# Recomputing xn and y from x for the gradients, LayerNorm of the first part on VectorE, and MLP weights loaded later

## The chip, the cores and the metric

The kernel runs on one core of a Trainium2 chip. The metric is the device time of one execution in microseconds (us); lower is better.

## The reference

A block of a network, forward and backward, in bf16. `xn = LN(x)`; an attention branch and a gated MLP branch both take `xn`; the MLP normalises once more (`y` below), and the result is `x + s * silu(m)`. The kernel returns the output and the gradients of all seven inputs.

```python
def _A_ref(x, wqkv, wo):            # B, S, D = 1, 2048, 512; H = 32 heads of 16
    qkv = (x @ wqkv).reshape(B, S, 3, H, Dh).transpose(2, 0, 3, 1, 4)
    q, k, v = qkv[0], qkv[1], qkv[2]
    scores = jnp.einsum("bhqd,bhkd->bhqk", q, k) * (Dh ** -0.5)
    p = _softmax(scores, axis=-1)
    o = jnp.einsum("bhqk,bhkd->bhqd", p, v)
    return o.transpose(0, 2, 1, 3).reshape(B, S, D) @ wo

def _B_ref(x, w1, b1, w2, b2):      # F = 1792
    y = _layernorm(x, axis=-1)
    h = _gelu(jnp.einsum("bsd,df->bsf", y, w1) + b1)
    return jnp.einsum("bsf,fd->bsd", h, w2) + b2

xn = _layernorm(x, axis=-1)
s = _A_ref(xn, A_wqkv, A_wo)
g = _silu(_B_ref(xn, B_w1, B_b1, B_w2, B_b2))
out = x + s * g                      # and jax.vjp of it with grad_out
```

## The kernel before

The 2048 rows are 16 tiles (t) of 128; four tiles make a group (g, or sc in the MLP). The order of the work on every engine is the order in which the program issues it (`manual_schedule`): each engine, and each queue from which an engine issues its DMAs, goes through its instructions one after the other, and an instruction that waits for a semaphore holds all behind it. The engines are TensorE (PE), VectorE (DVE), ScalarE (ACT), GpSimd (POOL) and SyncE (SP, which only issues DMAs). ScalarE computes and issues DMAs from the same queue.

There are three parts.

*The first part* (`phase_pre`, L37 to L279). SP loads x in four pieces; ScalarE issues the loads of wqkv and w1. `ln1(g)` computes the statistics of a group with `bn_stats` and `bn_aggr` on VectorE, a square root on ScalarE (L87) and a reciprocal on VectorE; `norm` (L91) then makes xn, on VectorE for group 0 and on GpSimd for groups 1 to 3. Group 0 is transposed by TensorE, the others by DMA transposes on SP (L108) into xnT. The loop over 16 tiles (L128) multiplies xnT with wqkv: three PSUM tiles pk, pv, pq per t, which ScalarE casts to NSall and NQ. GpSimd squares k and q (`sq`, L149, four buffers), VectorE sums the squares (L124). NSall has two halves that alternate by group, and each half is stored to NAT_s by SP after its fourth tile, NQ to NATQq_s. The hooks at L127 place `ln1(2)`, `ln1(3)` and the four `ln2` in this loop. `ln2(g)` stores xn to XN_s, makes y from xn, transposes y to yT and stores y to Y_s. At t = 3 ScalarE issues the loads of w2, b1 and b2, at t = 7 SP the transposing load of woT.

Then follows the MLP forward. `h1(sc)` (L185) makes 14 PSUM tiles from w1 and yT; VectorE adds b1 into h1row (six buffers), ScalarE applies gelu into hgT, SP stores every h1row to H1T_s and at the end hgT to HGT_s. `m_step(t)` multiplies hgT with w2 (ps_m), makes the gate and its slope (gB, stored to GB_s), the gradient dso and its projection with woT. Two groups of h1 run ahead of the first m_step.

*The attention core* (`attention_core`, L634) computes forward and backward of the 32 heads and leaves Oall and dQall in SBUF and dKVT_s in DRAM.

*The last part* (`phase3`, L347) makes the output and the gradients. First dWo from Oall and dso (ps_dwo, L434; four copies by ScalarE at L438 through three buffers). Then a loop over 16 tiles (L452): ps_so from oT and wo, two products on VectorE with the two halves of gb (dm_all, t1), the output on GpSimd (`ot`, with the tile xt of x), and dW of q from xn_all and dQall (L469). gb and xt are loaded by ScalarE's queue in `load_gbx`, three buffers each, two tiles ahead:

```python
                if t + 2 < NT:
                    load_gbx(t + 2)
```

xn_all is loaded from XN_s in four pieces before the loop (L428). After it come dW of k and v (L486), db2, and dW2 (L504 to L522), seven chunks of hidden units whose activations hgc are loaded by DMA transposes through two buffers; y_all is loaded from Y_s ahead of it (L501). The gradients through the MLP (`do_D`, `do_E`, with y_all in the LayerNorm backward), through LN (with xn_all) and dW1 (with y_all) end the program.

Of the kernel before, what the change touches and what calls it, by code (L numbers as in the profile page):

```python
# [9 lines left out]
f32 = mybir.dt.float32  # L10
ACT = mybir.ActivationFunctionType
ALU = mybir.AluOpType
# [4 lines left out]
NT = S // 128  # L17
# [19 lines left out]
def phase_pre(tc, k, A_x, A_wqkv, A_wo, B_w1, B_b1, B_w2, B_b2, grad_out):  # L37
    nc = tc.nc
# [3 lines left out]
    with ExitStack() as c1:  # L42
# [24 lines left out]
        with ExitStack() as c0:  # L67
# [7 lines left out]
            for i in (1, 2, 0):  # L75
                nc.scalar.dma_start(out=wqkv_sb[:, :, i * D:(i + 1) * D], in_=wv[:, :, i * D:(i + 1) * D])
            nc.scalar.dma_start(out=w1_sb[:], in_=B_w1.rearrange("(c p) f -> p c f", p=128))
            xn, y, st = {}, {}, {}

            def stats(g, src, rstd_all, tagn):  # L80
                s6 = wk0.tile([128, 4, nc.vector.BN_STATS_DIM], f32, name="ln_st")
                mv = wk0.tile([128, 4, nc.vector.BN_AGGR_DIM], f32, name="ln_mv")
                for i in range(4):
                    nc.vector.bn_stats(out=s6[:, i, :], in_=src[:, i, :])
                    nc.vector.bn_aggr(out=mv[:, i, :], in_=s6[:, i, :])
                rs = rstd_all[:, 4 * g:4 * g + 4]
                nc.scalar.activation(out=rs, in_=mv[:, :, 1], func=ACT.Sqrt, bias=k.eps_t[:], scale=1.0)  # L87
                nc.vector.reciprocal(out=rs, in_=rs)
                return mv, rs

            def norm(eng, dst, src, mv, rs):  # L91
# [3 lines left out]

            def ln1(g):
                src = x_all[:, 4 * g:4 * g + 4, :]
                mv, rs = stats(g, src, k.rstd1, "1")
                xn[g] = p0.tile([128, 4, D], bf16, name="xn", bufs=4)
                norm(nc.vector if g == 0 else nc.gpsimd, xn[g], src, mv, rs)  # L100
                if g == 0:
                    for i in range(4):
                        pt = psT.tile([128, IC, 128], bf16, name="tp_ps", tag="tp")
                        for b in range(IC):
                            nc.tensor.transpose(pt[:, b, :], xn[g][:, i, b * 128:(b + 1) * 128], k.ident_bf[:])
                        nc.scalar.copy(out=xnT[:, i, :, :], in_=pt[:])
                else:
                    nc.sync.dma_start_transpose(out=xnT[:, 4 * g:4 * g + 4].rearrange("c t m q -> c (t m) q"),  # L108
                                                in_=xn[g][:].rearrange("q t c -> q (t c)"))

            def ln2(g):
                nc.sync.dma_start(out=k.XN_s[g * 512:(g + 1) * 512, :].rearrange("(t p) d -> p t d", p=128), in_=xn[g][:])
                mv, rs = stats(g, xn[g], k.rstd2, "2")
                y[g] = p0.tile([128, 4, D], bf16, name="y", bufs=2)
                norm(nc.vector, y[g], xn[g], mv, rs)
                nc.sync.dma_start_transpose(out=yT[:, 4 * g:4 * g + 4].rearrange("c t m q -> c (t m) q"),
                                            in_=y[g][:].rearrange("q t c -> q (t c)"))
                nc.sync.dma_start(out=k.Y_s[g * 512:(g + 1) * 512, :].rearrange("(t p) d -> p t d", p=128), in_=y[g][:])

            sqs = {}  # L120

# [6 lines left out]
            for t in range(NT):  # L128
                i4 = t // 4
                if t % 4 == 0:  # L130
                    NQ = p0.tile([128, NPAIR, 4, 2, DH], bf16, name="NQ", bufs=2)
                ns = NSall[:, i4 % 2]
                ps3 = []
                for i in range(3):
                    off = (1, 2, 0)[i] * D
                    ps = psA.tile([128, 512], f32, name=("pk", "pv", "pq")[i], tag="mm")
                    for ic in range(IC):
                        nc.tensor.matmul(ps[:], lhsT=xnT[:, t, ic, :], rhs=wqkv_sb[:, ic, off:off + D], start=(ic == 0), stop=(ic == IC - 1))
# [4 lines left out]
                nc.scalar.copy(out=kk, in_=as_pairs(ps3[0]))  # L143
                nc.scalar.copy(out=ns[:, :, t % 4, :, 17:33], in_=as_pairs(ps3[1]))
                nc.scalar.activation(out=qq, in_=as_pairs(ps3[2]), func=ACT.Copy, scale=0.25)
                sqs[t] = []
                for dst, v in ((kn2, kk), (qn2, qq)):
                    sq = wk0.tile([128, H, DH], f32, name="sq", bufs=4)
                    nc.gpsimd.tensor_tensor(out=sq[:].rearrange("p (a j) c -> p a j c", j=2), in0=v, in1=v, op=ALU.mult)  # L149
                    sqs[t].append((dst, sq))  # L150
                for f in hooks.get(t, ()):
                    f()
                if t >= 1:
                    reduce_of(t - 1)
                if t % 4 == 3:
                    nc.sync.dma_start(out=k.NAT_s[:, :, t - 3:t + 1, :].rearrange("a p t c -> p a t c"), in_=ns.rearrange("p a t j c -> p a t (j c)"))
                    nc.sync.dma_start(out=k.NATQq_s[:, :, t - 3:t + 1, :].rearrange("a p t c -> p a t c"), in_=NQ[:].rearrange("p a t j c -> p a t (j c)"))
                if t == 3:
                    nc.scalar.dma_start(out=w2_sb[:], in_=B_w2.rearrange("(c p) d -> p c d", p=128))
                    nc.scalar.dma_start(out=b1_bf[:], in_=B_b1.rearrange("(c p) -> p c", p=128))  # L160
                    nc.scalar.dma_start(out=b2_bf[:], in_=B_b2.rearrange("(o d) -> o d", o=1).to_broadcast([128, D]))
                if t == 7:
                    nc.sync.dma_start_transpose(out=woT[:], in_=A_wo)
            reduce_of(NT - 1)
            nc.vector.tensor_copy(out=b1c[:], in_=b1_bf[:])
            nc.vector.tensor_copy(out=b2bc[:], in_=b2_bf[:])
# [10 lines left out]
        with ExitStack() as c0:  # L177
# [77 lines left out]
                m_mm(t)  # L255
            ops0 = pair_loads(nc, k, op0, op0["Pad"], 0)
            first = {9: ops0["plain"], 10: ops0["ck"], 11: ops0["tk"], 12: lambda: ops0["cq"](0, 4), 13: lambda: ops0["tq"](0, 4)}
            load_dot(0)
            load_dot(1)
            h1(0)  # L260
            h1(1)
            row_bound()
            for sc in range(4):
                for t in range(4 * sc, 4 * sc + 4):
                    m_step(t)
                    if t in first:
                        first[t]()
                if sc + 2 < 4:
                    h1(sc + 2)
            gate(NT - 1)  # L270
            slope_out(NT - 3, nc.gpsimd)
            slope_out(NT - 2, nc.gpsimd)
# [74 lines left out]
def phase3(ctx, tc, k, A_x, A_wqkv, A_wo, B_w1, B_w2, grad_out, out_0, out_1, out_2, out_3, out_4, out_5, out_6, out_7):  # L347
# [5 lines left out]
    with ExitStack() as c1:  # L353
# [23 lines left out]
        with ExitStack() as c2:  # L377
# [643 lines left out]
def full_kernel(ctx, tc, A_x, A_wqkv, A_wo, B_x, B_w1, B_b1, B_w2, B_b2, grad_out,  # L1021
# [9 lines left out]
    nc.vector.memset(k.eps_t[:], EPS)  # L1031
    k.rstd1 = persist.tile([128, NT], f32, name="rstd1")
    k.rstd2 = persist.tile([128, NT], f32, name="rstd2")
    k.ones_bf = persist.tile([128, 1], bf16, name="ones_bf")
    nc.vector.memset(k.ones_bf[:], 1.0)
    persist.tile([128, 192], mybir.dt.uint8, name="pad_to_256")

    def scratch(name, shape, dt=bf16):
        return tc.dram_tile(list(shape), dt, name=name)
    k.XN_s = scratch("XN_s", [S, D])  # L1040
    k.Y_s = scratch("Y_s", [S, D])
    k.DSO_s = scratch("DSO_s", [S, D])
    k.H1T_s = scratch("H1T_s", [F, S])
    k.HGT_s = scratch("HGT_s", [F, S])
# [82 lines left out]
```

## Time and profile before

| | us |
|---|---|
| median of 5 runs | 2373.32 |
| lowest, highest | 2365.41, 2394.01 |
| profiled execution, its time | 2383.65 |
| profiled execution, its span | 2381.9 |

| stretch of the profiled execution, us from the span's start | PE busy | DVE busy | ACT busy | POOL busy |
|---|---|---|---|---|
| 0 to 73.4 (qkv, LN) | 48.37 | 47.50 | 29.84 | 56.70 |
| 73.4 to 118.5 (h1 of two groups) | 29.30 | 26.32 | 18.59 | 4.81 |
| 118.5 to 211 (gate and the rest of h1) | 90.82 | 68.14 | 51.96 | 55.19 |
| 2021 to 2072.5 (so, dm, dW of q) | 34.73 | 20.33 | 3.84 | 17.31 |
| 2072.5 to 2101.7 (dW of k and v) | 29.20 | 0.00 | 5.54 | 1.15 |
| 2101.7 to 2166 (dW2) | 53.16 | 0.68 | 7.62 | 0.00 |

The profile is one execution. Times are from the start of its span. In a chain of waits each piece is a start, a duration and what ran; a DMA piece lasts from its issue to its landing. In the groups by line, "L93 POOL" is line 93 on GpSimd, the arrow leads from what was read to what was written, and numbers after "x" are counts. "ACTq" and "SPq" are DMA issues from those engines' queues. A line of waits gives who waited for whom, the total, the number of times and the longest.

### The profile page before, as it was taken

How to read it: one execution, taken by the hardware profiler on the slowest of the kernel's cores; microseconds unless marked ns; L12 is line 12 of the kernel's file. 1: busy time of each engine (PE TensorE's matmuls, PEld its weight loads, DVE VectorE, ACT ScalarE, POOL GpSimd, SP SyncE). 2: the span in 40 equal slices, each digit the busy share in tenths (PEclk: the TensorE clock that was granted, in tenths of full speed). 3: DMA queues.
4: the chain of work that ended last, by engine and by line, in shares of the span. 5: the costliest groups of instructions: out<-in, count | busy, mean ns of one | idle time of the engine just before them, and what ended most of it. 6: DMA issues, size and time to landing. Idle time of an engine off the chain costs nothing.

```text
span 2381.9 us, 47567 instructions
## 1 busy us (share of the span) xinstructions
PE 2216.9 (93%) x18320; PEld 734.0 (31%) x18320; DVE 1804.0 (76%) x3002; ACT 1812.6 (76%) x2098; POOL 1220.8 (51%) x1968
## 2 busy tenths in 40 slices
PE   5799999999999999999999999999999998789997
PEld 2343222222222222222222222222222223334446
DVE  5676898998698889979898988898887994304641
ACT  3465899998699889989998999999998995011231
POOL 7247456666266637565746566574746565200020
PEclk9898899998599889989998999999998999999999
DMA  6957999999799999999999999999999999999456
GB/s 196 282 198 204 224 233 249 240 241 233 170 223 248 242 203 241 239 230 234 236 242 233 239 249 235 231 244 242 239 236 228 235 235 252 255 260 255 147 90 129
DMA packets 1769958, 538.29 MB, mean 226 GB/s; under 512 B 1682545, under 2 KB 1755394, under 8 KB 1769730
## 3 DMA queue, kind: packets, MB, share of 16 engines
q1 hardware_dynamic: 1718274, 469.95, 97.0%
q10 hardware_dynamic: 39136, 37.90, 5.6%
q0 software_dynamic: 12320, 27.41, 3.9%
q8 instruction: 143, 2.34, 0.4%
q14 instruction: 85, 0.70, 0.1%
HBM read 52.17 MB, written 62.53 MB: 48 GB/s over the span
## 4 chain that ended last, share of the span: by engine, by line
PE 49%; ACT 21%; DMA 13%; POOL 7%; issue 4%; DVE 4%; SPq 0%; ACTq 0%; POOLq 0%; DVEq 0%
ACT e L789 10%; PE d L767 9%; ACT eg L781 9%; PE s L755 8%; PE X L825 8%; DMA tg<-eg 7%; PE X L837 5%; PE Z L933 3%; PE X L849 2%; PE ps_dy L563 2%; PE ps_dhg L548 2%; PE ps_h L190 2%; PE ps_dw L509 2%; PE ps_m L202 1%; DMA hgc<-HGT_s 1%
## 5 line engine op out<-in xcount | busy, mean ns | idle before, releaser
L799 DVE TENSOR_TENSOR eg<-d,eg 128x512 bf16<-128x512 f32 x2048 | 1351.5, 687 | 219.1 <-PE d L767 77.9
L781 ACT ACTIVATE eg<-s 128x1024 bf16<-128x1024 f32 x1024 | 1041.6, 1035 | 96.0 <-PE d L767 65.8
L767 PE MATMUL d<-QDT,KVT 32*128 32x512 bf16 x2048 | 824.3, 403 | 0.7 <-DVE eg L799 0.6
L789 ACT ACTIVATE e<-t 128x1024 bf16<-128x1024 f32 x640 | 663.4, 1037 | 53.5 <-PE t L741 51.4
L755 PE MATMUL s<-QDT,KVT 32*128 32x512 bf16 x2048 | 418.0, 403 | 42.9 <-ACT eg L781 39.9
L837 PE MATMUL X<-eg,NAT 128*32 128x512 bf16 x2048 | 423.4, 411 | 0.0
L825 PE MATMUL X<-eg,Lc 128*32 128x512 bf16 x2048 | 422.8, 410 | 0.0
L849 PE MATMUL X<-eg,NAT 128*17 128x512 bf16 x2048 | 416.0, 403 | 0.0
L767 PEld LDWEIGHTS <-KVT 32*128 32x128 bf16 x2048 | 186.6, 91 | 359.0 <-issue 359.0
L921 PE MATMUL Z<-e,W 128*32 128x512 bf16 x1280 | 261.4, 404 | 20.4 <-POOL W L888 19.0
L741 PE MATMUL t<-KVT,QDT 32*128 32x512 bf16 x1280 | 260.5, 401 | 2.1 <-ACT eg L781 1.5
L882 POOL TENSOR_TENSOR W<-NATQd,rL 128x128 bf16<-128x128 bf16 x64 | 25.9, 405 | 378.3 <-DVE rL L866 378.3
L933 PE MATMUL Z<-tg,W 128*32 128x512 bf16 x2048 | 212.4, 399 | 0.0
L755 PEld LDWEIGHTS <-KVT 32*128 32x128 bf16 x2048 | 117.5, 91 | 305.4 <-issue 303.7
L825 PEld LDWEIGHTS <-Lc 128*32 128x32 bf16 x2048 | 99.2, 94 | 291.7 <-issue 291.7
L688 POOL TENSOR_TENSOR bg_v<-bg_t 128x512 f32<-128x512 f32 x56 | 58.0, 1036 | 201.9 <-ACT bg_t L703 201.5
L921 PE MATMUL Z<-tg,W 128*32 128x512 bf16 x768 | 157.8, 408 | 0.0
L837 PEld LDWEIGHTS <-NAT 128*32 128x32 bf16 x2048 | 99.5, 94 | 173.9 <-issue 173.9
L344 POOL TENSOR_TENSOR dx<-lnb_prod,lnb_dy 128x512 bf16<-128x512 f32 x16 | 20.9, 1312 | 235.1 <-DVE lnb_prod L343 234.4
L947 DVE TENSOR_TENSOR acc<-Z,acc 128x512 f32<-128x512 f32 x192 | 130.6, 680 | 10.7 <-PE Z L933 10.7
L921 PEld LDWEIGHTS <-W 128*32 128x32 bf16 x2048 | 108.8, 93 | 47.1 <-POOL W L888 23.3
L849 PEld LDWEIGHTS <-NAT 128*17 128x17 bf16 x2048 | 93.0, 88 | 61.8 <-issue 61.8
(161 smaller groups left out, 2753.7 us busy)
## 6 DMA issues: line engine op xcount, KB each, us to landing
H1T_s<-h1row SPq DMA_DIRECT2D x56, 128.0 KB, 1.8
HGT_s<-hgT SPq DMA_DIRECT2D x4, 1792.0 KB, 7.4
bg_x<-H1T_s POOLq DMA_DIRECT2D x56, 128.0 KB, 5.3
GP_s<-bg_m POOLq DMA_DIRECT2D x56, 128.0 KB, 5.6
gp<-GP_s ACTq DMA_DIRECT2D x8, 896.0 KB, 8.6
DH1T_s<-dh1T SPq DMA_DIRECT2D x4, 1792.0 KB, 9.5
NAT_s<-NSall SPq DMA_DIRECT2D x4, 1056.0 KB, 7.0
NAT<-NAT_s POOLq DMA_DIRECT2D x16, 264.0 KB, 5.9
```

The lines of the kernel that those rows point to most:

```text
L741: nc.tensor.matmul(t[:, hj, :], lhsT=op["QDT"][r:r + 32, q0:q0 + 128], rhs=op["KVT"][r:r + 32, kc * 512:(kc + 1) * 512], start=True, stop= ...
L755: nc.tensor.matmul(s[:, hj, :], lhsT=op["KVT"][r:r + 32, kb * 128:(kb + 1) * 128], rhs=op["QDT"][r:r + 32, qc * 512:(qc + 1) * 512], start ...
L767: nc.tensor.matmul(d[:], lhsT=op["KVT"][r:r + 32, kb * 128:(kb + 1) * 128], rhs=op["QDT"][r:r + 32, qc * 512:(qc + 1) * 512], start=True, ...
L781: nc.scalar.activation(out=cur["eg"][1][:, :, kb % 4, :, :].rearrange("k b h q -> k h b q"), in_=st_s.pop(g)[:].rearrange("k h (b q) -> k ...
L789: nc.scalar.activation(out=e[:], in_=st_t.pop(g)[:], func=ACT.Exp)
L799: nc.vector.tensor_tensor(out=gts[:, kb % 4, hj, :].rearrange("k (b q) -> k b q", b=4), in0=ds[hj][:].rearrange("k (b q) -> k b q", b=4), ...
L825: nc.tensor.matmul(X[64 + 32 * hj:96 + 32 * hj, :], lhsT=Lc[:], rhs=et[:, :, kb % 4, hj, :], start=(kb == 0), stop=False, skip_group_check ...
L837: nc.tensor.matmul(X[32 * hj:32 * hj + 32, :], lhsT=NATt[:, kb, hj, 1:33], rhs=et[:, :, kb % 4, hj, :], start=(kb == 0), stop=(kb == 15), ...
L849: nc.tensor.matmul(X[64 + 32 * hj:64 + 32 * hj + 17, :], lhsT=NATt[:, kb, hj, 0:17], rhs=gts[:, kb % 4, hj, :], start=False, stop=(kb == 1 ...
L921: nc.tensor.matmul(Z[32 * hj:32 * hj + 32, :], lhsT=blk[j]["W1"][:, qb, hj, :], rhs=ev[:, hj], start=(i == 0), stop=False, tile_position=( ...
L933: nc.tensor.matmul(Z[c:c + 32, :], lhsT=blk[j]["W2"][:, qb, hj, :], rhs=gv[:, :, hj, qb, :], start=(i == 1), stop=(i >= 2), tile_position= ...
L947: nc.vector.tensor_tensor(out=av, in0=Z[:], in1=av, op=ALU.add)
```

## The change

In the first part all four groups of xn are made on VectorE. `stats` also keeps, for every row, minus the mean times the reciprocal deviation (`nmr1`, `nmr2`). xn and y are no longer stored to DRAM. b1 and b2 are loaded from ScalarE's queue at the very start. w2 and woT are no longer loaded inside the qkv loop: SP issues w2 after `h1(0)`, then the first load of grad_out, then woT, then `h1(1)` and the second load of grad_out. A one-column Exp on ScalarE stands behind the last m_step.

In the last part xn_all is not loaded; `make_xn(t)` makes tile t with one ScalarE activation from xt, a tile that the loop loads anyway, and it is issued one iteration ahead of its use. y_all is made tile by tile from xn_all by ScalarE during the dW2 chunks. The small tiles nmr1 and nmr2 take their space from a pad.

```diff
             nc.scalar.dma_start(out=w1_sb[:], in_=B_w1.rearrange("(c p) f -> p c f", p=128))
+            nc.scalar.dma_start(out=b1_bf[:], in_=B_b1.rearrange("(c p) -> p c", p=128))
+            nc.scalar.dma_start(out=b2_bf[:], in_=B_b2.rearrange("(o d) -> o d", o=1).to_broadcast([128, D]))
...
                 nc.vector.reciprocal(out=rs, in_=rs)
+                nc.vector.scalar_tensor_tensor(out=nmr_all[:, 4 * g:4 * g + 4], in0=mv[:, :, 0], scalar=-1.0, in1=rs, op0=ALU.mult, op1=ALU.mult)
...
-                norm(nc.vector if g == 0 else nc.gpsimd, xn[g], src, mv, rs)
+                norm(nc.vector, xn[g], src, mv, rs)
...
             def ln2(g):
-                nc.sync.dma_start(out=k.XN_s[g * 512:(g + 1) * 512, :].rearrange("(t p) d -> p t d", p=128), in_=xn[g][:])
...
-                nc.sync.dma_start(out=k.Y_s[g * 512:(g + 1) * 512, :].rearrange("(t p) d -> p t d", p=128), in_=y[g][:])
...
-                if t == 3:
-                    nc.scalar.dma_start(out=w2_sb[:], in_=B_w2.rearrange("(c p) d -> p c d", p=128))
-                    nc.scalar.dma_start(out=b1_bf[:], in_=B_b1.rearrange("(c p) -> p c", p=128))
-                    nc.scalar.dma_start(out=b2_bf[:], in_=B_b2.rearrange("(o d) -> o d", o=1).to_broadcast([128, D]))
-                if t == 7:
-                    nc.sync.dma_start_transpose(out=woT[:], in_=A_wo)
...
+            h1(0)
+            nc.sync.dma_start(out=w2_sb[:], in_=B_w2.rearrange("(c p) d -> p c d", p=128))
             load_dot(0)
+            nc.sync.dma_start_transpose(out=woT[:], in_=A_wo)
+            h1(1)
             load_dot(1)
-            h1(0)
-            h1(1)
             row_bound()
...
+            nc.scalar.activation(out=kmax2[:, 0:1], in_=k.eps_t[:], func=ACT.Exp)
             gate(NT - 1)
...
-            xnv = k.XN_s.rearrange("(t p) d -> p t d", p=128)
-            for i in range(4):
-                nc.scalar.dma_start(out=xn_all[:, 4 * i:4 * i + 4, :], in_=xnv[:, 4 * i:4 * i + 4, :])
+
+            def make_xn(t):
+                nc.scalar.activation(out=xn_all[:, t, :], in_=gbx[t][1][:], func=ACT.Identity, bias=k.nmr1[:, t:t + 1], scale=k.rstd1[:, t:t + 1])
...
+            make_xn(0)
             for t in range(NT):
+                if t + 1 < NT:
+                    make_xn(t + 1)
                 ps = psA.tile([128, D], f32, name="ps_so", tag="mm")
...
-            nc.scalar.dma_start(out=y_all[:], in_=k.Y_s.rearrange("(t p) d -> p t d", p=128))
...
+                if i < 6:
+                    for t in range(3 * i, min(3 * i + 3, NT)):
+                        nc.scalar.activation(out=y_all[:, t, :], in_=xn_all[:, t, :], func=ACT.Identity, bias=k.nmr2[:, t:t + 1], scale=k.rstd2[:, t:t + 1])
```

More of the change, by code (lines that the diff above doesn't have):

```diff
@@ L77, in phase_pre, with stats @@
             nc.scalar.dma_start(out=w1_sb[:], in_=B_w1.rearrange("(c p) f -> p c f", p=128))
+            nc.scalar.dma_start(out=b1_bf[:], in_=B_b1.rearrange("(c p) -> p c", p=128))
+            nc.scalar.dma_start(out=b2_bf[:], in_=B_b2.rearrange("(o d) -> o d", o=1).to_broadcast([128, D]))
             xn, y, st = {}, {}, {}
-            def stats(g, src, rstd_all, tagn):
+            def stats(g, src, rstd_all, nmr_all):
                 s6 = wk0.tile([128, 4, nc.vector.BN_STATS_DIM], f32, name="ln_st")
@@ L97, in ln1 @@
                 src = x_all[:, 4 * g:4 * g + 4, :]
-                mv, rs = stats(g, src, k.rstd1, "1")
+                mv, rs = stats(g, src, k.rstd1, k.nmr1)
                 xn[g] = p0.tile([128, 4, D], bf16, name="xn", bufs=4)
-                norm(nc.vector if g == 0 else nc.gpsimd, xn[g], src, mv, rs)
+                norm(nc.vector, xn[g], src, mv, rs)
                 if g == 0:
@@ L111, in ln2 @@
             def ln2(g):
-                nc.sync.dma_start(out=k.XN_s[g * 512:(g + 1) * 512, :].rearrange("(t p) d -> p t d", p=128), in_=xn[g][:])
-                mv, rs = stats(g, xn[g], k.rstd2, "2")
+                mv, rs = stats(g, xn[g], k.rstd2, k.nmr2)
                 y[g] = p0.tile([128, 4, D], bf16, name="y", bufs=2)
@@ L1033, in full_kernel @@
     k.rstd2 = persist.tile([128, NT], f32, name="rstd2")
+    k.nmr1 = persist.tile([128, NT], f32, name="nmr1")
+    k.nmr2 = persist.tile([128, NT], f32, name="nmr2")
     k.ones_bf = persist.tile([128, 1], bf16, name="ones_bf")
     nc.vector.memset(k.ones_bf[:], 1.0)
-    persist.tile([128, 192], mybir.dt.uint8, name="pad_to_256")
+    persist.tile([128, 64], mybir.dt.uint8, name="pad_to_256")
     def scratch(name, shape, dt=bf16):
         return tc.dram_tile(list(shape), dt, name=name)
-    k.XN_s = scratch("XN_s", [S, D])
-    k.Y_s = scratch("Y_s", [S, D])
     k.DSO_s = scratch("DSO_s", [S, D])
```

## The prediction

> **What bounds the kernel now.** I read the page first: 40 slices of 59.5 us. The attention core fills slices 4 to 34, and the change touches nothing in it. What is at stake lies before about 211 us and after about 2007 us, so I then took the chain of waits and the timeline for those two stretches, and after that the groups by tile.
>
> First stretch, from the chain of waits (start, duration, what):
>
> ```profile
> 15.01 4.84 POOL xn L93 x3
> ...
> 29.34 6.20 POOL xn L93 x3
> ...
> 41.57 6.22 POOL xn L93 x3
> ...
> 95.47 5.57 DMA H1T_s<-h1row
> 101.16 0.76 DVE h1row L193
> 101.97 16.67 PE ps_h L190 x64
> ```
>
> The reader sees GpSimd's normalisation of groups 1 to 3 as the pacemaker up to 50 us, and then a store of h1row for which VectorE and TensorE wait. The waits of these two windows name the losses (waiter, releaser: total, times, longest):
>
> ```profile
> ACT NSall L143 <- DMA NAT_s<-NSall: 9.2, 1, 9.2
> ACT NSall L143 <- DMA w_sb<-in_B_w_dram: 6.5, 1, 6.5
> PE pk L138 <- DMA xnT<-xn: 2.9, 1, 2.9
> DVE h1row L193 <- DMA H1T_s<-h1row: 16.6, 2, 14.5
> ```
>
> The 6.5 us is ScalarE's own queue. The timeline has it issuing b2 from 32.67 to 38.06 us, with the casts of the qkv tiles behind it:
>
> ```profile
> 32.67 5.39 ACTq L161 DMA_DIRECT2D b_bf<-in_B_b_dram  x1
> ```
>
> The 14.5 us is SP's queue: XN_s at 81.75, yT, Y_s, NAT_s, NATQq_s and two dot loads are issued one after the other, and the first H1T_s store goes only at 95.47 us and lands 5.6 us later. The six h1row buffers are full meanwhile.
>
> Second stretch: loop over 16 tiles with so, dm and the dW of q (L452 to L474). By tile gb, and the waits:
>
> ```profile
> L400 ACTq DMA_DIRECT2D gb<-GB_s x16: 326/373/686, 2005.4 to 2065.9; - x16
>   DMA gb<-GB_s: 27.7, 11
> DMA to landing us min/median/max: 3.1/4.7/10.2
> ```
>
> For tile xt the last line reads
>
> ```profile
> DMA to landing us min/median/max: 2.6/4.8/10.5
> ```
>
> So the loop waits 11 times for its loads of gb, and the windows show the DMA engines full there (share 1.16, 256 GB/s from 2021 to 2072.5) while TensorE is busy for 34.7 of 51.5 us. Up to three pairs gb/xt are in flight. gb(2) is issued at 2028.33, gb(15) at 2065.88: 37.55 us for 13 iterations, 2.89 each. The last matmul of L486 ends at 2098.17.
>
> **What the Trainium skill says.** "DMA: Bandwidth & Descriptors", section Rules for kernel authors, says to issue a DMA early and wait for its semaphore late, so that its fixed cost overlaps; its section Anatomy of one DMA puts that fixed cost, on the path through GpSimd, at about 2 us. This trace agrees: the unloaded dout loads of 128 KB land 1.9 to 2.1 us after issue. "GPSIMD Engine Reference", section Engine selection, calls GpSimd roughly line-rate for one-input operations and gives elementwise work to VectorE; here the same tensor_scalar of 128x512 bf16 takes 2086 ns on POOL and 404 ns on DVE, so the measurement decides. "ScalarE: Activation LUTs", section What ACT_TABLE_LOAD costs, prices a table load at 1283 ns; the trace shows 1283 ns at L87, L194 and L781.
>
> **Part 1: the first part (L67 to L196).** Removed: 12 POOL operations of 2.08 us, eight stores of 512 KB on SP, and w2, b1, b2 and woT from inside the qkv loop. VectorE gets 12 norms of 0.40 (in fours 1.4 to 1.5 us, so +4.5 us) and eight tiny products (+0.8). VectorE is then the bound of the qkv part. From 5.9 to 82.6 us it spent 76.7 us, of which about 19.5 idle (kn and qn wait 14.6 for POOL's sq, rstd 4.5), so 57.2 of work; with +5.3 and 8 waits of 0.36 to 0.6 us for the square root that stay (4.5) it is 67, and the first h1row comes at 5.9 + 67 = 73 us instead of 82.6. TensorE doesn't set this: 48 groups of 0.865 us from 12.4 end near 54, or near 62 where ScalarE's copies queue behind a square root that waits for VectorE. NAT_s of group 0 is no longer behind the transpose of xn(3), so the 9.2 us go too; that is inside the 67.
>
> The stall of h1(0) shrinks. SP has only yT(3), NAT_s(3) and NATQq_s(3) ahead of the first H1T_s (0.45 + 2.9 + 2.9 us from about 69), so I take 1 to 3 us, and h1(0) ends at about 82 (six rows buffered, eight more at 0.87). Then SP issues HGT_s, w2 (1792 KB), dot(0) and woT: 0.4 + 2.9 + 2.9 + 4.95, by what NATQq_s, its successor and woT showed. The rows of h1(1) queue behind these until 94, with a landing of 2 to 4 us. Six rows are covered by their buffers and six by PSUM; after that TensorE stands some 5 us, and h1(1) ends near 98 to 99. The first ps_m started at 118.5. Gain 19.5 us. If SP is quicker the stall vanishes and the gain is 24.
>
> What is added ahead: b1 and b2 now stand on ScalarE's queue before its first table load (3.46 us) and before the square root at 9.24. b2's issue took 5.39 behind w2 and b1. Where it returns by 8 us it costs nothing; where it waits until w1 has largely drained (w1 landed 15.4 us after its issue at 2.41), ScalarE starts near 15 and all shifts by 6 to 7. I take 1.5 us, ends 0 and 7. Part 1: -18, ends -11 and -24. From 118.5 to 211 TensorE is busy 90.8 of 92.5 us, so the shift passes through whole.
>
> **Part 2: the Exp at L267.** It puts the table load (1.28 at 211.87, on the chain) ahead, but ScalarE has only about 0.5 us idle there and dsoT and ND queue behind it. -1, ends 0 and -1.3.
>
> **Part 3: xn_all from xt.** Removed: four loads of 512 KB at 2012.5. That lets the dKVT_s store land earlier (7.6 us after 2014.2 now, 5.3 is its median), and the four dwo copies with the ring of three follow: gb(2) goes near 2025.8 instead of 2028.33.
>
> Added: make_xn(t+1), on ScalarE, in front of load_gbx(t+2). It waits for xt(t+1), which was issued in the iteration before. Queued behind that wait on ScalarE are exactly the loads of gb and xt of t+2. So at most one pair is in flight where it was up to three, and the period becomes a chain: issue gb 0.37, gap 0.08, xt from issue to landing, 0.05, activation 0.7 (the 128x512 bf16 ones take 0.63, the one with pointer scale in f32 0.80), gap 0.05. With landing 2.6 (the lowest) it is 3.85; with the median 4.8 it is 6.0. One pair alone queues less behind itself, but the transposes of dm and dKV and the output stores remain; I take 3.0 as a rule (period 4.25), and two slow landings beside the dKV transposes as at 2047.8 lift the mean to 4.4. Thirteen periods are 57.2: gb(15) at 2083.0, xt(15) lands at 2086.4, make_xn and dwq(15) 1.7, then 128 matmuls of 0.2155 = 27.6: 2115.7. Against 2098.17: +17.6, say +18; ends +9 and +40. The 2 MB taken off the DMA engines doesn't pay here, since latency is the limit now.
>
> **Part 4: y_all from xn_all.** Sixteen activations of 0.7 (11 us) on ScalarE, which is busy only 7.6 of the 64 us of the dW2 stage: hidden, else 2 us each round. Removed: a 2 MB load at 2099.75, just before hgc(2) is issued (2108.76, landing after 12.6 where the median is 7.8), for which TensorE waits:
>
> ```profile
> PE ps_dw L509 <- DMA hgc<-HGT_s: 11.1, 3, 5.8
> ```
>
> 2 MB at 271 GB/s are 7.7 us; the 5.8 us wait mostly goes, what is late next is hgc(4) behind w2T. -5, ends -1 and -8.
>
> **Sum.** -18 - 1 + 18 - 5 = -6, against the profiled execution (2383.65, span 2381.9, i.e. 1.75 around it). That one lies 10.3 above the median of the five runs, 2373.32, and none of the parts depends on it; I put the -6 on the median: 2367.
>
> **Rivals.**
> A, slower: the serial loads decide. One mechanism, at L452: landing stays at the median 4.8 because transposes fill the engines (share 1.16 speaks for it; the smaller own queue against), period 6.0. Then part 3 is +40 and the sum -18 - 1 + 40 - 5 = +16: 2389. It decides from a period of 4.86 us, where part 3 reaches +24 and the change is worth nothing.
> B, clearly faster: landing 2.6 (period 3.85: part 3 about +10), no stall of h1(1) (part 1 -23) and dW2 -6: -20, so 2353. For it: three xt landings at 2.6 to 3.0 in the loop; against: those fell between transposes.
> C, no change: LN moves as planned, but b2's issue holds ScalarE at the start until about 15 us, part 1 -11: sum +1, 2374. For it: b2 returned at 38.06, just when w2 landed (38.7); against: four loads of 512 KB were issued at the start in 0.5 us each with none landed.
>
> **How the numbers follow.** Forecast 0.45, A 0.20, B 0.20, C 0.15. The range 2344 to 2392 takes B with its margin and A's centre; outside stay A's far end and B's. A measurement here tells about 1% (24 us) from no change. Faster by more: about half of B, a tail of the forecast and runs spread by 29 us: 0.18; slower by more: the upper part of A and a little else: 0.09; within: 0.73.
>
> **What would show it.** First ps_m at about 100 us (right: 96 to 107); first h1row near 73 and no wait over 4 us for H1T_s in h1(0), but one in h1(1); VectorE the releaser for ScalarE's square roots. In the loop ScalarE waiting for xt about 13 times, gb issues 4.2 to 4.6 us apart and the L486 group ending about 18 us later relative to L434's start. hgc waits of ps_dw down from 11.1 to about 5. The forecast is wrong if loads still overlap in the loop (period near 2.9), if ScalarE's first operation comes after 12 us, or if the attention core itself changes length.

## The result and the profile after

The change makes no difference that this measurement can tell from none. The kernel after took 2366.07 us (median of 44 runs, 2338.58 to 2392.53), the kernel before 2374.67 us (79 runs, 2339.17 to 2403.9), and the ratio of the two is 0.9987 with a 95% interval of 0.9969 to 1.0005, that is -3 us (-7 to +1). The ratio is formed from undisturbed runs alone, so here and below it need not equal the quotient of the medians. The forecast was 2367 us, with a change within 1% as the likeliest outcome. It came out, but two of its parts were off by 10 and 12 us in opposite directions, and most of what follows is about these two.

The profiled execution of after has a span of 2354.3 us and a time of 2356.32, 27 us less than that of before. Most of this is not the change. From the first matmul of the attention core to the first one of `ps_dwo` it took 1771.9 us, against 1795.7. In the windows of before and then of after (stretch, its length, busy time of PE, PEld, DVE, ACT and POOL, granted TensorE clock, DMA share, GB/s)

```profile
211.20:800.00 588.80, 566.71 (x5038) 158.12 (x5037) 495.67 (x780) 525.79 (x570) 331.63 (x568) 0.90 1.12 228
```

```profile
204.40:800.00 595.60, 567.09 (x5250) 163.19 (x5249) 514.45 (x813) 545.83 (x593) 354.36 (x608) 0.95 1.17 236
```

the reader sees TensorE busy for the same 567 us, with more matmuls done in it, at a granted clock of 0.95 instead of 0.90. Kernels below that differ only in the queue or the order of two bias loads have cores of 1753.5 and 1798.0 us, so the core's length says nothing on the change. A straight line through all runs for which a clock is listed, with one slope and an offset for each kernel, falls by 16.4 us per 0.01 of granted clock and leaves 3.8 us of scatter; at a clock of 0.945 it gives 2374.1 for before and 2371.2 for after, a difference of -2.9. The line takes the clock as given; whether a kernel itself shifts the clock that it is granted was not tested. I therefore compare stage by stage outside the core. Stages in us, all read from the groups by tile (here and below a stage that ends with a group of matmuls is read to the start of the last one, 0.4 us before its end; the forecast for the first row has the 1.5 us for b1 and b2 in it):

| stage | before | after | difference | forecast |
|---|---|---|---|---|
| start to first h1row | 82.6 | 77.7 | -4.9 | -8.1 |
| first h1row to first ps_m | 35.9 | 32.8 | -3.1 | -10 |
| first ps_m to first matmul of the core | 92.7 | 93.9 | +1.2 | -1 |
| first ps_dwo to gb(2) | 21.4 | 16.6 | -4.8 | -2.5 |
| gb(2) to gb(15) | 37.6 | 50.7 | +13.1 | +19.7 |
| gb(15) to the end of L487 (L486 before) | 31.9 | 32.0 | +0.1 | +0.4 |
| dW2 | 68.1 | 62.0 | -6.1 | -5 |
| the rest | 216.0 | 216.7 | +0.7 | 0 |
| all outside the core | 586.2 | 582.4 | -3.8 | -6.5 (-6 as rounded) |

The lines that answer to those of before: first the chain of waits at the start (start, duration, what).

```profile
0.72 5.43 DMA wqkv_sb<-in_A_wqkv_dram
...
6.59 9.41 ACTq L79
16.03 1.28 ACT L89
...
18.03 1.29 DVE xn L96 x4
```

L79 is the load of b2. GpSimd's normalisation has gone from the chain; ahead of everything now stands ScalarE's queue, which spends 9.41 us on issuing b2. The waits from 0 to 60 us (waiter, releaser: total, times, longest) say who stood behind it:

```profile
ACT L89 <- issue: 16.0, 1, 16.0
ACT rstd L89 <- DVE ln_mv L87: 14.6, 5, 4.4
...
DVE rstd L90 <- ACT rstd L89: 10.5, 6, 8.7
```

VectorE waited 8.7 us for a square root that could not start. The waits for w_sb, NAT_s and xnT of before are gone. From 60 to 122 us the store of h1row is still waited for:

```profile
DVE h1row L188 <- DMA H1T_s<-h1row: 13.3, 2, 12.2
PE ps_h L185 <- DVE h1row L188: 12.7, 2, 8.7
```

The 12.2 us is in `h1(1)` now; TensorE stands for 8.7 of them. SP's timeline shows three long issues between two rows:

```profile
90.05 1.74 SPq L254 DMA_DIRECT2D w_sb<-in_B_w_dram  x1
91.88 4.70 SPq L178 DMA_DIRECT2D dot<-in_grad_out_dram  x1
96.63 7.00 SPq L256 DMA_TRANSPOSE woT<-in_A_wo_dram  x1
```

In the loop of the last part, the gb and xt groups by tile and the waits have

```profile
L398 ACTq DMA_DIRECT2D gb<-GB_s x16: 326/326/565, 1974.4 to 2043.6; - x16
  DMA gb<-GB_s: 14.1, 6
DMA to landing us min/median/max: 2.5/2.9/5.0
```

```profile
L426 ACT ACTIVATE xn_all<-xt,nmr,rstd x16: 797/813/814, 1992.8 to 2046.5; 128x512 bf16<-128x512 bf16 x16
...
DMA to landing us min/median/max: 2.4/2.8/6.1
```

```profile
ACT xn_all L426 <- DMA xt<-in_A_x_dram: 35.0, 12, 5.8
...
PE ps_dwq L470 <- ACT xn_all L426: 18.9, 9, 4.7
```

Waits for gb have halved (27.7 before), a landing takes 2.8 to 2.9 us instead of 4.7 to 4.8, and yet the 13 periods take 13 us longer: ScalarE waits 12 times for xt before it can issue the next loads. The timeline shows two links of this chain; the gb of the next tile is issued just after the activation that waited has begun, and not after it has ended:

```profile
2000.43 0.81 ACT L426 ACTIVATE xn_all<-xt,nmr,rstd 128x512 bf16<-128x512 bf16 x1 [2.66 <-DMA xt<-in_A_x_dram]
2000.49 0.33 ACTq L398 DMA_DIRECT2D gb<-GB_s  x1
2000.93 0.37 ACTq L400 DMA_DIRECT2D xt<-in_A_x_dram  x1
...
2005.29 0.81 ACT L426 ACTIVATE xn_all<-xt,nmr,rstd 128x512 bf16<-128x512 bf16 x1 [4.05 <-DMA xt<-in_A_x_dram]
```

The DMA engines, whose share was 1.15 to 1.16 in this loop before, have slack (the number before the last, 0.82; the one ahead of it is the granted clock):

```profile
1991.00:2048.20 57.20, 36.55 (x129) 13.05 (x128) 20.07 (x32) 14.20 (x19) 17.31 (x15) 0.85 0.82 205
```

and TensorE is busy for 37 of 57 us. In the dW2 stage the wait for hgc has shrunk from 11.1 us to

```profile
PE ps_dw L509 <- DMA hgc<-HGT_s: 7.3, 4, 5.2
```

That is 3.8 of the 6.1 us. The other 2.3 are TensorE itself, which in this stage is busy for 54.69 us at a granted clock of 0.94, against 56.96 at 0.90 before; busy time multiplied by clock comes to the same 51.4 and 51.3. By this estimate, that part is the clock's and not the change's.

### The profile page after: what moved, and what is told of

Its sections match the earlier page's. It is cut to its first block, busy times and chain, and to the rows that moved or that the text cites. A ratio compares the mean times of both kernels' runs of the same rounds, so it can differ in the third digit from the quotient of the medians.

```text
span 2354.3 us, 47577 instructions
## 1 busy us (share of the span) xinstructions
PE 2192.0 (93%) x18320; PEld 731.8 (31%) x18320; DVE 1804.9 (77%) x3022; ACT 1835.4 (78%) x2131; POOL 1196.4 (51%) x1956
## 4 chain that ended last, share of the span: by engine, by line
PE 50%; ACT 22%; DMA 10%; POOL 6%; DVE 6%; issue 4%; ACTq 1%; SPq 0%; POOLq 0%; DVEq 0%
ACT e L792 10%; ACT eg L784 9%; PE d L770 9%; PE s L758 8%; PE X L828 8%; DMA tg<-eg 5%; PE X L840 4%; PE Z L936 3%; PE X L852 2%; PE ps_dy L566 2%; PE ps_dhg L551 2%; PE ps_h L185 2%; PE Z L924 1%; DMA hgc<-HGT_s 1%; PE ps_dw L509 1%
## 5 line engine op out<-in xcount | busy, mean ns | idle before, releaser
L770 PE MATMUL d<-QDT,KVT 32*128 32x512 bf16 x2048 | 809.8, 396 | 1.0 <-DVE eg L802 0.9
L758 PE MATMUL s<-QDT,KVT 32*128 32x512 bf16 x2048 | 410.6, 396 | 41.8 <-ACT eg L784 38.8
L840 PE MATMUL X<-eg,NAT 128*32 128x512 bf16 x2048 | 416.0, 403 | 0.0
L828 PE MATMUL X<-eg,Lc 128*32 128x512 bf16 x2048 | 414.5, 402 | 0.0
L852 PE MATMUL X<-eg,NAT 128*17 128x512 bf16 x2048 | 408.9, 396 | 0.0
L828 PEld LDWEIGHTS <-Lc 128*32 128x32 bf16 x2048 | 98.8, 93 | 285.8 <-issue 285.8
```

The lines of the kernel that those rows point to most:

```text
L758: nc.tensor.matmul(s[:, hj, :], lhsT=op["KVT"][r:r + 32, kb * 128:(kb + 1) * 128], rhs=op["QDT"][r:r + 32, qc * 512:(qc + 1) * 512], start ...
L770: nc.tensor.matmul(d[:], lhsT=op["KVT"][r:r + 32, kb * 128:(kb + 1) * 128], rhs=op["QDT"][r:r + 32, qc * 512:(qc + 1) * 512], start=True, ...
L828: nc.tensor.matmul(X[64 + 32 * hj:96 + 32 * hj, :], lhsT=Lc[:], rhs=et[:, :, kb % 4, hj, :], start=(kb == 0), stop=False, skip_group_check ...
L840: nc.tensor.matmul(X[32 * hj:32 * hj + 32, :], lhsT=NATt[:, kb, hj, 1:33], rhs=et[:, :, kb % 4, hj, :], start=(kb == 0), stop=(kb == 15), ...
L852: nc.tensor.matmul(X[64 + 32 * hj:64 + 32 * hj + 17, :], lhsT=NATt[:, kb, hj, 0:17], rhs=gts[:, kb % 4, hj, :], start=False, stop=(kb == 1 ...
```

## The experiments

Each kernel is the one after with one edit, unless said otherwise. "Outside" is the span without the attention core. The same stage in kernels that leave it alone shows what one profile is worth: the stretch from `ps_dwo` to the end of L487 took 97.1 to 100.7 us in the six of them with an unchanged loop.

**The start: b2's issue.** b1 (1792 elements of two bytes, each a piece of its own, 14 to a partition) and b2 (one row copied to all 128 partitions) go to GpSimd's queue.

```diff
-nc.scalar.dma_start(out=b1_bf[:], ...)
-nc.scalar.dma_start(out=b2_bf[:], ...)
+nc.gpsimd.dma_start(out=b1_bf[:], ...)
+nc.gpsimd.dma_start(out=b2_bf[:], ...)
```

> The changed kernel with b1 and b2 loaded from GpSimd's queue instead of ScalarE's, at the same place at the start. Theory: b2's issue (9.4 us) is what holds ScalarE until 16.0, so the table load goes back to near 3.5, the first square root to about 9.2, and the whole first part shifts: first h1row from 77.7 to about 70 to 71, first ps_m from 110.5 to about 103. Rival 1 (VectorE has slack later in the qkv part, so that a late start is made up for): first h1row stays above 76. Rival 2 (1792 two-byte pieces and x or wqkv share the DMA engines, so that the loads of x and wqkv themselves are late): the first square root still comes after 14.

The first h1row came at 69.6 us instead of 77.7, the first ps_m at 102.4 instead of 110.5, the core at 196.5 instead of 204.4; GpSimd's queue spent 1.29 and 0.58 us on the two issues. The hold cost 8 us and not the 12.6 by which ScalarE's first operation had moved (3.46 us before, 16.03 after). The square root that it feeds moved by 8.1 only, from 9.24 to 17.33: in the kernel before, ScalarE waits there 4.49 us for VectorE's statistics. The second run keeps both on ScalarE and exchanges them.

```diff
+nc.scalar.dma_start(out=b2_bf[:], ...)
 nc.scalar.dma_start(out=b1_bf[:], ...)
-nc.scalar.dma_start(out=b2_bf[:], ...)
```

> The changed kernel with b2 loaded before b1, both still from ScalarE's queue. Theory: the 9.4 us come about because the DMA that stands behind the 1792 two-byte pieces of b1 can't be issued until these have gone out; with b1 last nothing stands behind it but computing, so ScalarE starts by about 7 to 8 us and first h1row comes at 70 to 72. Rival (any DMA issued behind w1 waits for w1 to drain): b2's issue or b1's takes 6 us or more again, ScalarE starts after 13 and first h1row stays at 76 to 78.

```profile
6.25 0.35 ACTq L78 DMA_DIRECT2D b_bf<-in_B_b_dram  x1
6.64 0.45 ACTq L79 DMA_DIRECT2D b_bf<-in_B_b_dram  x1
7.12 1.28 ACT L89 ACT_TABLE_LOAD   x1 [7.12 <-DMA wqkv_sb<-in_A_wqkv_dram]
```

This is the timeline at the start (L78 is b2 here, L79 is b1). The same two loads now take 0.35 and 0.45 us to issue, and the first h1row comes at 68.7. So neither load is slow to issue by itself, and standing behind w1 is not the reason: what costs 9.4 us is to be the next issue behind b1 on this queue. That it is b1's 1792 pieces that hold the queue is the likely reason; only the order was tested. The first of the two starts at 6.2 us in either order, about when the first load of wqkv has landed, but this costs nothing: the table load ends at 8.40, and the square root waits until 9.09 for VectorE.

**The first part: LN on VectorE, alone.** The norms of groups 1 to 3 go back to GpSimd; all else of the change stays.

```diff
-norm(nc.vector, xn[g], src, mv, rs)
+norm(nc.vector if g == 0 else nc.gpsimd, xn[g], src, mv, rs)
```

> The changed kernel with xn of groups 1 to 3 made on GpSimd again (the LayerNorm part undone alone). Theory (GpSimd's 8.3 us per group in front of its squares was a pacemaker of the qkv part, and VectorE with 4.5 us more is a better one): first h1row from 77.7 to 82 to 86. Rival (VectorE is the only bound, so its 4.5 us come back): first h1row at 73 to 76.

The first h1row came at 91.2 us, the core at 219.0 instead of 204.4. The waits from 0 to 80 us have, with b2's hold at the start passed on to GpSimd in the first line,

```profile
POOL xn L96 <- DVE rstd L90: 18.3, 1, 18.3
...
ACT NSall L144 <- DMA NAT_s<-NSall: 9.5, 1, 9.5
```

The NAT_s wait of before is back. VectorE's norms are worth 14.6 us at the core's start, more than was expected; the rest of the change in the first part, by itself, made it 7.8 us slower than before (219.0 against 211.2), about what b2's hold costs.

**The stall in h1(1).** The first load of grad_out and woT move behind `h1(1)`; w2 stays ahead of it.

```diff
 nc.sync.dma_start(out=w2_sb[:], ...)
+h1(1)
 load_dot(0)
 nc.sync.dma_start_transpose(out=woT[:], in_=A_wo)
-h1(1)
```

> The changed kernel with load_dot(0) and woT issued after h1(1) instead of before it; w2 stays between h1(0) and h1(1). Theory (the 12.2 us for which h1row of h1(1) waits come from SP's queue, where dot(0) took 4.7 and woT 7.0 us to issue): the wait falls below 2 us, TensorE has no stall in h1(1), and the first ps_m comes 8 to 9 us earlier, near 102. Rival (the wait is for the data of w2 and HGT_s to drain through the DMA engines, so the H1T_s stores land late whatever stands in the queue): still 8 us or more of wait. A second rival: the time comes back in the m steps, since dot(0) or woT is late there; then the first s of the attention core stays at 204.

The first ps_m came at 107.4 us, 3 us earlier and not 8 or 9. The waits of the kernel from 60 to 215 us:

```profile
DVE h1row L188 <- DMA H1T_s<-h1row: 10.2, 2, 9.1
...
DVE dso L208 <- DMA dot<-in_grad_out_dram: 5.4, 1, 5.4
```

and the last line of tile h1row from 88 to 93 us:

```profile
DMA to landing us min/median/max: 1.8/1.9/11.2
```

The rival came true. SP's queue still stood:

```profile
91.86 4.70 SPq L190 DMA_DIRECT2D H1T_s<-h1row  x1
```

The issue behind HGT_s and w2 (3.6 MB together) takes the same 4.70 us whether it is a load of 512 KB of grad_out or, as here, a store of 128 KB, and the store landed 11.2 us after its issue began. So what costs is what stands ahead, w2 and HGT_s; only woT's 7.00 us have gone, and TensorE's longest wait fell from 8.7 to 5.6. The second rival came true as well: the load of grad_out came too late for `dso`, and the core started at 208.9, 4.5 us later than in the kernel after. What goes behind `h1(0)` therefore has to move ahead, not back; the last three kernels do that.

**y.** Y_s is stored and loaded again as before; xn is still made from x.

```diff
+nc.sync.dma_start(out=k.Y_s[g * 512:(g + 1) * 512, :]..., in_=y[g][:])
...
+nc.scalar.dma_start(out=y_all[:], in_=k.Y_s.rearrange("(t p) d -> p t d", p=128))
...
-                    for t in range(3 * i, min(3 * i + 3, NT)):
-                        nc.scalar.activation(out=y_all[:, t, :], in_=xn_all[:, t, :], ...)
```

> The changed kernel with y stored to DRAM and loaded again in one piece ahead of dW2, without the sixteen activations (the y part undone alone). Theory (the 2 MB load stood in the way of hgc(2)): from the end of the L487 group to the end of the ps_dw group of dW2 67 to 69 us instead of 62.0. Rival (the 6 us came from something else, as the granted clock or the gp loads): 61 to 64. The stores of y on SP's queue cost the first part 0 to 3 us.

The dW2 stage took 69.2 us instead of 62.0, and its waits have

```profile
PE ps_dw L511 <- DMA hgc<-HGT_s: 12.0, 2, 6.8
```

The 2 MB load of y delays hgc: of the 7.2 us, 4.7 are this wait, and TensorE is busy for 1.9 us more (56.56 against 54.69). The activations that replace the load are hidden. In the first part the stores cost 2.4 us at the first ps_m and 3.4 at the core's start.

**xn: what the loop loses, and to what.** First the loads are issued ahead of the activation that waits.

```diff
-if t + 1 < NT:
-    make_xn(t + 1)
 ps = psA.tile([128, D], f32, name="ps_so", tag="mm")
...
     load_gbx(t + 2)
+if t + 1 < NT:
+    make_xn(t + 1)
```

> The changed kernel with make_xn(t+1) issued after load_gbx(t+2) instead of before it; same activations, same transfers. Theory (one pair of loads in flight because the loads stand behind an activation that waits for the pair before): gb(2) to gb(15) takes 34 to 40 us instead of 50.7 (13 periods of 2.6 to 3.1 instead of 3.9), and the matmuls of L487 end 11 to 16 us earlier after ps_dwo starts than the 99.7 of the changed kernel. Rival (the sixteen activations or the DMA engines set the pace): 48 us or more, unchanged.

gb(2) to gb(15) took 42.1 us instead of 50.7: two thirds of the 13 us come back, not all, and the expectation of 34 to 40 was missed. The stretch from `ps_dwo` to the end of L487 took 92.4 us instead of 99.3, 6.9 less where 11 to 16 had been expected. In the next kernel the activation of tile t is issued in iteration t itself, behind the loads of t+2.

```diff
-make_xn(0)
...
-if t + 1 < NT:
-    make_xn(t + 1)
...
     load_gbx(t + 2)
+nc.scalar.activation(out=xn_all[:, t, :], in_=xt[:], func=ACT.Identity, bias=k.nmr1[:, t:t + 1], scale=k.rstd1[:, t:t + 1])
```

> The changed kernel with the activation of tile t issued in iteration t after the loads of t+2, so that the loads queue behind an activation that waits for xt(t), whose buffer the next load needs anyway. Theory (the number of pairs in flight sets the pace: one in the changed kernel 50.7 us from gb(2) to gb(15), two with the load first 42.1): up to three in flight, 34 to 39 us, and ps_dwo to the end of dW of k and v at 84 to 89 us instead of 99.3. Rival (at 42 the DMA engines or TensorE's chain through xn_all set the pace): 41 us or more.

It took 41.6 us, in the rival's range, and the stretch 93.2. Waits of the last stretch:

```profile
ACT xn_all L464 <- POOL ot L460: 20.0, 7, 5.0
...
PE ps_dwq L468 <- ACT xn_all L464: 16.1, 11, 3.9
```

The wait has only changed its name. A load of xt may be issued when GpSimd has read the tile that it overwrites; ScalarE stands there 7 times, and the activation for which TensorE waits is behind it. Where one queue both computes and loads, each waits for the other's condition. So xn was taken off that queue: VectorE makes it, one tile ahead, after its two products.

```diff
-    nc.scalar.activation(out=xn_all[:, t, :], in_=gbx[t][1][:], func=ACT.Identity, bias=k.nmr1[:, t:t + 1], scale=k.rstd1[:, t:t + 1])
+    nc.vector.tensor_scalar(out=xn_all[:, t, :], in0=gbx[t][1][:], scalar1=k.rstd1[:, t:t + 1], scalar2=k.nmr1[:, t:t + 1], op0=ALU.mult, op1=ALU.add)
```

> The changed kernel with xn of the last part made by VectorE, one tile ahead and after the two products of tile t, so that ScalarE's queue holds nothing but the loads there. Theory (what costs is only what the loads queue behind): gb(2) to gb(15) at 30 to 38 us, at or below the 37.6 of the kernel before, since 2 MB of loads are gone, and ps_dwo to the end of dW of k and v at 80 to 89 us instead of 99.3. Rival (with ScalarE freed the transposes of dKV and dm still hold the loads, or the product chain does): 40 us or more, as in the two other orders (42.1 and 41.6).

gb(2) to gb(15) took 37.8 us, the 37.6 of before, and the stretch from `ps_dwo` to the end of L487 87.4 us instead of 99.3. VectorE now waits for xt itself (18.5 us, 10 times), but no load stands behind it. Its operation is also shorter, 0.41 us against 0.81, and this run does not separate the two. Last, xn is stored and loaded as before, and nothing is recomputed for it.

```diff
+nc.sync.dma_start(out=k.XN_s[g * 512:(g + 1) * 512, :]..., in_=xn[g][:])
...
+for i in range(4):
+    nc.scalar.dma_start(out=xn_all[:, 4 * i:4 * i + 4, :], in_=xnv[:, 4 * i:4 * i + 4, :])
-make_xn(0)
...
-    make_xn(t + 1)
```

> The changed kernel with xn stored to DRAM and loaded again before the loop (the xn part undone alone). Theory: the loop goes back to 36 to 40 us from gb(2) to gb(15), gb(2) comes 3 to 5 us later, so ps_dwo to the end of dW of k and v is at 90 to 93 us instead of 99.3; in the first part the four stores on SP cost 0 to 4 us at the first ps_m. Rival (the loop is longer for another reason, as the lower granted clock or the placement of buffers): 47 us or more.

gb(2) to gb(15) took 33.6 us and the whole stretch 84.9; outside the core the kernel took 571.7 us, 10.7 less than the kernel after. The store of xn cost 0.9 us at the first ps_m and 1.8 at the core's start. By this pair of profiles, recomputing xn as the change does it loses about 11 us that the store and the loads did not; how far this depends on the pair is said further down.

**Three combinations.** All have b2 ahead of b1, and w2 (on ScalarE, at t = 3) and woT (on SP, at t = 7) in the qkv loop again:

```diff
+if t == 3:
+    nc.scalar.dma_start(out=w2_sb[:], ...)
+if t == 7:
+    nc.sync.dma_start_transpose(out=woT[:], in_=A_wo)
...
 h1(0)
-nc.sync.dma_start(out=w2_sb[:], ...)
 load_dot(0)
-nc.sync.dma_start_transpose(out=woT[:], in_=A_wo)
```

The first adds to this the activation in iteration t, behind the loads.

> The changed kernel with three edits: b2 loaded before b1 at the start; w2 issued by ScalarE at t = 3 and woT by SP at t = 7 of the qkv loop, as before the change; the activation of xn in iteration t after the loads of t+2. Theory: 9 us from the start of ScalarE, 8 to 10 us from h1(1), whose stores then have neither w2 nor woT ahead of them (first ps_m at 90 to 94), 10 to 14 us from the loop: together 27 to 33 us below the changed kernel outside the attention core (549 to 555 us), ratio to the kernel before 0.984 to 0.988. Rival (what is gained early comes back as a wait for dots, hgT or the transposes): outside the attention core 560 or more.

It has the first ps_m at 92.8 us as expected, 17.7 earlier than the kernel after, and the core at 190.8, so 4 us of it are given back before the core; TensorE's transposes wait 3.7 us for dso there, 0.9 in the kernel after. The loop took 47.5 us where the same loop alone had taken 41.6, and the stretch from `ps_dwo` to the end of L487 99.4, as in the kernel after: the gain of the new order is not seen here. Outside: 573.5 us, short of the 549 to 555 expected and within the rival's 560 or more. In five timed rounds it took 2349.68 us against 2373.66, a ratio of 0.9884 (0.9828 to 0.9941).

The second makes xn on VectorE instead.

> The changed kernel with b2 before b1, w2 at t = 3 and woT at t = 7 as before the change, and xn of the last part on VectorE. Theory: first s of the attention core near 191 as with the first two edits alone, the loop at 30 to 38 us, so 555 to 563 us outside the attention core (586.2 before, 582.4 in the changed kernel) and a ratio to the kernel before of 0.984 to 0.991. Rival (the loop gives back what it gains in dW2 or in the wait for the transposes of dKV): 567 or more.

Outside the core it took 563.5 us, the least of all, just above the 555 to 563 expected, with the core again from 190.8 and 91.5 us from `ps_dwo` to the end of L487; the loop took 40.0, not 30 to 38. But timed, 2356.88 against 2384.44 us in the medians, the ratio is 0.9989 (0.9898 to 1.0081), where 0.984 to 0.991 was expected.

The third stores and loads xn as before.

> The changed kernel with b2 before b1, w2 at t = 3 and woT at t = 7 as before the change, and xn through DRAM as before the change; y recomputed and LayerNorm on VectorE stay. Theory (the recomputation of xn is the one part that loses, some 11 us in a trace, and the other two edits gain about 13 up to the attention core): first s near 192, ps_dwo to the end of dW of k and v at 84 to 88 us, 553 to 562 us outside the attention core against 586.2 before and 582.4 changed, ratio to the kernel before 0.985 to 0.992. Rival (the stores of xn on SP's queue between the other transfers cost what the loop gains): 566 or more outside the core.

Loop 34.9 us, but gb(2) comes 21.5 us after `ps_dwo` as in the kernel before, and the stretch takes 92.7, not 84 to 88. Outside: 569.3 us, in the range of the rival. The ratio is 0.9994 (0.9959 to 1.003), 2357.35 against 2375.06 us in the medians of 22 and 27 runs.

So the ratio shows a gain for the first of the three alone. But it compares runs at whatever clock they were granted. In the first, the runs compared had a mean clock of 0.953 for the combination and 0.946 for before, which at 16.4 us per 0.01 accounts for an estimated 11 of the 27 us. In the other two it stood the other way, 0.943 against 0.954 (three runs of before) and 0.946 against 0.954. The straight line, read at one clock (0.945), puts the three at 2356.7, 2353.5 and 2358.6 us, that is 17.4, 20.6 and 15.5 below before, and the stages outside the core at 12.7, 22.7 and 16.9 below it. These two ways agree with each other, and with none of the three ratios. That all three gain some 15 us is thus likely and not settled.

## Why the prediction was right, and where it was wrong

The sum held (-6 forecast, -3.8 outside the core in the profiles, -3 by the ratio). Its parts did not.

**Part 1 and 2, forecast -19, measured -6.8.** The step "b1 and b2 on ScalarE's queue: I take 1.5 us, ends 0 and 7" failed. The hold itself was named, in rival C, with the draining of w1 or w2 as its cause, and was set aside because loads of 512 KB had been issued in 0.5 us each. Both the cause and the comparison by size were wrong: with b2 ahead of b1 the two are issued behind w1 in 0.35 and 0.45 us, and b2's 5.39 us in the kernel before were spent behind b1 as well. ScalarE's first operation came at 16.03 us, beyond the 12 that the forecast gave as a sign against itself; removing the hold gained 8 to 9 us. The term of VectorE's work was good: 73 us was forecast without b2, and 69.6 and 68.7 were measured once the hold was gone. The second miss was the stall of TensorE in `h1(1)`, "some 5 us", which was 8.7 (12.2 for VectorE): the issues of w2, dot(0) and woT took 1.74, 4.70 and 7.00 us where 2.9, 2.9 and 4.95 had been added, and in the kernel with dot(0) and woT moved back a store behind HGT_s and w2 landed after 11.2 us where 2 to 4 had been taken. Of the -1 for the Exp nothing is seen: the stage with it took 1.2 us longer. No kernel left it out alone, so its own effect stays open.

**Part 3, forecast +18, measured +8.4.** The mechanism was right: 12 waits of ScalarE for xt (13 forecast), gb and xt of the next tile behind them, TensorE behind xn. Issuing the loads ahead of the wait gave two thirds of it back. The mis-sized term is the period, 4.4 us forecast and 3.90 measured (50.7/13), and the step in it that failed is the activation: the chain has 0.7 us for it and 0.05 for the gap behind it, but the lines above show gb issued at 2000.49, 0.06 us after the start of the activation that waited (2000.43). The loads do not wait for the activation to end, so its 0.81 us are no part of the period. Over the 13 periods the time from xt's issue to the next activation has a mean of 3.36 us, and the two issues take the other 0.54. In the forecast these two came to 3.20 (a landing of 3.15 on average and a gap) and 0.45. So the landing was taken somewhat too short and not too long: its median is 2.8, but a few late ones, up to 6.1, lift the mean. Rival A, which needed a period above 4.86 us, is thereby out; rival B's 3.85 was nearer, though by a landing of 2.6 plus the activation. Against the kernel before, gb(2) came 4.8 us earlier where 2.5 was forecast.

The page "DMA: Bandwidth & Descriptors" of the Trainium skill, section Rules for kernel authors, was read in the prediction for its rule to issue early and wait late. This loop bears it out from the other side: with the same loads issued behind the activation that waits, instead of ahead of it, 13 tiles took 50.7 us and not 42.1. The same section says that spreading DMAs over the engines that issue them brings no bandwidth and only saves their issue time; the GpSimd run agrees in the second point, since the 8 us it gained were issue time, and no run here tests the first. The dout loads that the prediction set beside that page's 2 us are issued from ScalarE's queue, not GpSimd's, so their 1.9 to 2.1 us do not bear on that figure.

**Part 4, forecast -5, measured -6.1**, and 7.2 with y's load back. The mechanism was right: hgc was late behind y, and the activations are hidden. Its size was 3.8 us in the one comparison and 4.7 in the other; most of the rest is TensorE at another granted clock.

**The core.** The forecast would be wrong, it said, if the core changed its length. It did in the two profiled executions, by 23.8 us, but this goes with the granted clock: two kernels that differ only in b1 and b2 have cores 44.5 us apart, at 0.963 and 0.941.

Why the sum was right nonetheless: 12 us too much gain in the first part stood against 10 us too much loss in the loop. That is luck, and the agreement within 1 us of the median must not be read as precision.

Two things stay open. The loop of the first combination took 47.5 us and the same loop by itself 41.6, one profile each. In it ScalarE waits 26.2 us for GpSimd's `ot` instead of 20.0, and the granted clock is 0.80 instead of 0.92; whether the clock is the cause is not shown. And with xn loaded from DRAM the stretch from `ps_dwo` to the end of L487 took 84.9, 90.9 and 92.7 us in three kernels; the loss by recomputing against their mean of 89.5 is 9 us (the six kernels with the loop as changed have a mean of 98.8), but against a single one it may come out at 6 or at 14.

## What to carry to other kernels

Before moving arithmetic to "an engine that is idle", look at what that engine's queue issues: an operation that waits for a load also holds every load behind it, and the saved transfer is paid for in latency. Put a load made of many tiny pieces last in its queue ahead of compute; here that alone gained 9 us. In the sum of a chain, count an operation only where the next step waits for its end; here the loads waited for the activation's start alone. Check a forecast by its stages, outside the stretch where the granted clock sets the time, since a sum can agree while its parts cancel.

## What the runs showed of the hardware that was not expected

- The issue of a 128 KB load behind one of 1792 two-byte pieces held ScalarE's queue for 9.41 us; issued ahead of it 0.35 us, and the one of two-byte pieces itself then 0.45. On GpSimd's queue the two took 1.29 and 0.58.
- SP's issue behind two transfers of 1.8 MB each took 4.70 us, both for a load of 512 KB and for a store of 128 KB.
- In the loop the load of gb that stands in ScalarE's queue behind an activation was issued 0.06 to 0.09 us after that activation's start for 12 of 13 tiles (gb(3) to gb(15)), and after 0.5 for the other; it never waited for the 0.81 us to end.
- ScalarE's Identity of 128x512 bf16 with scale and bias read from a column took 0.81 us, where its operations of this size without such columns, bf16 to bf16, took 0.57 to 0.63 in the kernel before.
- The whole time falls by 16.4 us, 0.7%, per 0.01 of granted TensorE clock, in runs of the same kernel. The runs of the kernel after spread over 54 us and those of before over 65, more than all that was at stake here.
- A store of 128 KB that lands in 1.9 us as a rule took 11.2 behind 3.6 MB of other transfers from the same queue, 4.70 of them in its issue.
